# Early weight slots and tokens turned by VectorE in a one-core attention and mixture kernel

## The chip, the cores and the metric

One core of a Trainium2 chip runs the whole program. The metric is the device time of one execution in microseconds; lower is better. TensorE (PE) multiplies, VectorE (DVE), ScalarE (ACT) and GpSimd (POOL) do the work between, and SyncE (SP) issues most of the transfers, which 16 DMA engines carry out.

## The reference, cut to what matters

```python
scores = scale * np.matmul(q, k.transpose(0, 1, 3, 2)) - np.log(S)   # 4 batches, 12 heads, S = 448
x = (1.0 / (1.0 + np.exp(-scores))) @ v       # joined heads: 1792 tokens x 768
x = ((x @ w_a) * (x @ w_b)) @ w_out           # w_a, w_b: 768 x 1536; w_out: 1536 x 768
logits = x @ phi                              # 32 slots, 4 for each of 8 experts
d = softmax over all tokens of logits         # columns
slot_input = d.T @ x
slot_out[e] = relu(slot_input[e] @ w1[e]) @ w2[e]    # w1, w2: 8 x 768 x 1024 and 8 x 1024 x 768
out = softmax over slots of logits @ slot_out
```

All is 32-bit. The experts' weights w1 and w2 are 25.2 MB each; everything else is smaller.

## The kernel before

Four batches of 448 tokens pass through in order. `att` computes attention; `ab(0)` computes a * b for the first batch, between the steps of attention. For the two middle batches `unit(u)` (12 units of 7 block products, line 843) forms both batches' a and b at once; `put` multiplies them. `ab(B - 1)` does the last batch by itself: for each of 12 column blocks fc, and for a and b (i = 0, 1), 18 matmuls of 128 x 448 (line 660) in three sets of six. So it has 72 steps, counted by i in the main loop, with a `yield` after each set. w_a and w_b were rewritten to DRAM (`ab32`); each half block of 384 KB is loaded by `load_w` (line 542), rounded by DVE (line 550) and its low part formed by POOL (line 551). The load of fc 4's first half is the first that `run["load"]` asks for after the main loop has set up its buffers.

The product a * b of a column block lies with features on partitions (`gT`). To be summed over tokens it must lie with tokens on partitions (`gk`). `group(b, gi)` does this for four column blocks: for gi = 0 and 1 with DVE transposes of 32 x 32 pieces (line 603), then `store_gk` writes the result to DRAM (`gk32`, runs of 512 B) and `reload_gk` reads it back in token order; for gi = 2 with PE transposes (line 624) and copies out of PSUM (line 626), without DRAM. `LG(b)` then forms a batch's logits, their exponentials (`weights`) and, in `dg` (line 936), adds d.T @ (a * b) to `acc`. w_out is applied once, to that small sum. `fill` is a list of such pieces of side work; `fill_step` puts the next one into the program between sets of matmuls.

The experts' weights stream through a ring of slots of 8 KB per partition. `pump` takes the next of 61 pieces from `queue` (5 of w_out, 24 of w1 at 1 MB, 32 of w2 at 768 KB) and a free slot, and issues the load on SP; `done` frees a slot after its matmuls and pumps again. There are 22 slots in all: 17 in pool `e1` (its first six serve as reload buffers and work space until LG(1) and LG(2) are through), one `gkp`, and four `e2`, which open when `ab(B - 1)` has ended; the very last of them holds the last batch's gi = 2 tokens until `dg` of that batch. `e1` is opened at step 6 of `ab(B - 1)` in the memory of the block products, and the first `pump` comes at step 12. SP issues strictly in program order; an SP instruction that waits holds all loads behind it.

After `last_LG` comes the product with w_out (line 1229: four strips of 32 columns of PE, one for each fc modulo 4), then w1 (1249), w2 (1275) and the output (1301, 1323).

Of the kernel before, what the change touches and what calls it, by code (L numbers as in the profile page):

```python
# [20 lines left out]
C = 4  # L21
# [4 lines left out]
STARTS = (0, 128, 256, S - 128)  # L26
NP = H // 2
NE1, NE2 = 17, 4
# [12 lines left out]
def body(ctx, tc, q, k, v, w_a, w_b, w_out, phi, w1, w2, out):  # L41
# [5 lines left out]
    ps_ctx, ab_ctx, x0_ctx, cv_ctx, at_ctx, cp_ctx, xb_ctx = (ctx.enter_context(ExitStack()) for _ in range(7))  # L47
# [49 lines left out]
    gk32 = drp.tile([B, 2, S, 512], F32, name="gk32")  # L97
# [193 lines left out]
    def raw_x(b, kk):  # L291

        if b == 1 or (b == 3 and kk < 5):
            nm = f"t{kk if b == 1 else 6 + kk}"
            return x1p.tile([128, S], F32, tag=nm, name=nm)
        if b == 2 and kk >= 3:
            while fill:
                fill_step()
            return gT_all[kk - 1]
        nm = f"r{kk}" if b == 2 else "x3t"  # L300
        return pools["cp"].tile([128, S], F32, tag=nm, name=nm)
# [233 lines left out]
    LAST = 2 * (NCH - KF)  # L535

# [49 lines left out]

    def group(b, gi, evac=(act.copy, dve.tensor_copy) * 2):
# [12 lines left out]
        if gi < 2:  # L600
            turned = gk[:, :4 * S].rearrange("p (n f) -> p n f", f=128)
            for j in range(4):
                dve.transpose(turned[:, :, 32 * j:32 * j + 32], gT[b, 4 * gi + j].rearrange("p (n t) -> p n t", t=32))
                yield
                if b < B - 1:
# [32 lines left out]
    def store_gk(b, gi, turned, eng=sp, rows=range(4)):  # L638
        dst = gk32[b, gi].rearrange("(n t) (r f) -> r t n f", t=32, r=4)
        for r in rows:  # L640
            eng.dma_start(out=dst[r], in_=turned[32 * r:32 * r + 32])

    def reload_gk(b, gi, t):
        t = t.rearrange("p (c n) -> p c n", c=C)
        src = gk32[b, gi]
        sp.dma_start(out=t[:, :3], in_=src[:384].rearrange("(c p) n -> p c n", c=3))
        sp.dma_start(out=t[64:, 3], in_=src[384:])
        gtok[b, gi] = t

    def ab(b):  # L650
        for fc in range(KF):
# [3 lines left out]
            for i in range(2):  # L655
                wh, wl = ws[i]
                t = ps_tile("ab", [128, S], 2)
                for s, (w, xi) in enumerate(((wh, b == B - 1), (wh, b < B - 1), (wl, 0))):
# [23 lines left out]
                if LAST <= 2 * n + 2 < 2 * NCH:  # L682
# [8 lines left out]
                    if x + 1 == 2 * NCH:  # L691
                        run.pop("wr")
                        open_slots(run["e1"], [0])
                        pump()
# [11 lines left out]
    def load_u(u):  # L706
        if u > NU + 1:
            return
        t = pools["cp"].tile([128, 1536], F32, tag="wr", name="wr", bufs=2)
# [88 lines left out]
    def g_slot(u, q, n):  # L798
        k = (u // 2 * 4 + q) % 12
        while gslots.get(k) in live:  # L800
            fill_step()
        gslots[k] = n
        live.add(n)
        if k < 4:
            return gT_all[k + 1]
        if k < 8:
            return pools["xb"].tile([128, S], F32, tag=f"g{k}", name=f"g{k}")
        nm = ("r0", "r1", "r2", "x3t")[k - 8]
        return pools["cp"].tile([128, S], F32, tag=nm, name=nm)
# [3 lines left out]
    def p_tile():  # L813
        k = tmp[0] % 6
        tmp[0] += 1
        if 0 < tmp[0] - 1 < 4:
            nm = f"g{3 + k}"
            return pools["xb"].tile([128, S], F32, tag=nm, name=nm)
# [4 lines left out]
    def unit(u):  # L823
# [40 lines left out]
        if u % 4 == 3:  # L864
            fill.append(group(2, u // 4))
            fill.append(group(1, u // 4))
# [6 lines left out]
    def logits(b):  # L873
# [25 lines left out]
        ls, d = run["lsd"]  # L899
        if not b:  # L900
            dve.tensor_copy(ls, lf)
            run["exp"] = lambda: act.activation(d, ls, AF.Exp, bias=nm, accum_out=sm)
            run["s"] = sm
            return
        act.activation(d, lf, AF.Exp, bias=nm, accum_out=sm)
# [16 lines left out]
    def weights(d, dst):  # L922
        t = ms((128, C, NS))
        for c in range(C):
# [3 lines left out]
    def dg(b, dtok, gp, groups):  # L928

        kept = groups[0] == 2  # L930
        gk = gtok[b, groups[0]][:, None] if len(groups) == 1 else gk_01.rearrange("p g (c n) -> p g c n", c=C)
        o = gp.rearrange("p (g n) -> p g n", g=3)[:, groups[0]:groups[-1] + 1]
        for c in range(C):
            rows = slice(64 * (c == C - 1), 128)
            for j in range(4):
                pe.matmul(o[32 * j:32 * j + 32], dtok[rows, c], gk[rows, :, c, j * 128:(j + 1) * 128] if kept  # L936
                          else gk[rows, 0, c].rearrange("p (r j f) -> p j r f", r=4, j=4)[:, j],
# [18 lines left out]
    def rest_LG(b, dtok):  # L956
        weights(run["lsd"][1], dtok)
# [3 lines left out]
        for groups in ((0,), (1,), (2,)):  # L961
            dg(b, dtok, gp, groups)
# [5 lines left out]
        if b == B - 3:  # L968
            open_slots(run["e1"], [2, 3])
        elif b == B - 2:  # L970
            run.pop("lsd2")
            open_slots(run["e1"], [1, 4, 5])
# [13 lines left out]
    def last_LG():  # L986
# [9 lines left out]
        weights(run["lsd"][1], dtok)  # L996
# [4 lines left out]
        for groups in ((0,), (1,), (2,)):  # L1001
            dg(B - 1, dtok, gp, groups)
# [56 lines left out]
    def pump():  # L1059
# [6 lines left out]
        if what[0] == "wo":  # L1066
            i = what[1]
            if i < 3:
                t = t.rearrange("p (a n) -> p a n", a=4)
                src = out32[:, 4 * i:4 * i + 4, :512]  # L1070
            else:
                t = t[:, :6 * 256].rearrange("p (a n) -> p a n", a=6)
                src = out32[:, 6 * (i - 3):6 * (i - 3) + 6, 512:]
            sp.dma_start(out=t, in_=src)
# [55 lines left out]
    x0_ctx.close()  # L1130
    pools["cp"] = cp_ctx.enter_context(tc.tile_pool(name="cp", bufs=1, side="left"))
# [44 lines left out]
    load_w(LAST + 5)  # L1176
    for i, frac in enumerate(ab(B - 1)):
# [3 lines left out]
        if i == 6:  # L1181
            while fill:
                fill_step()
            cp_ctx.close()
            xb_ctx.close()
            e1 = run["e1"] = ctx.enter_context(tc.tile_pool(name="e1", bufs=1, side="right"))
            run["lsd2"] = e1.tile([128, 2048], F32, tag="e11", name="lsd2")
            run["wr"] = e1.tile([128, 2048], F32, tag="e10", name="wr")
            load_w(LAST + 6)
            load_w(LAST + 7)  # L1190
            for x in range(4):
                nm = f"e1{2 + x}"
                reload_gk(1 + x // 2, x % 2, e1.tile([128, 2048], F32, tag=nm, name=nm))
            open_slots(e1, range(6, NE1))
# [6 lines left out]
        if i >= 12 and i % 3 == 0:  # L1201
            pump()
# [20 lines left out]
    for what in order0:  # L1223
        i = what[1]
        h, n, f0 = (0, 4, 4 * i) if i < 3 else (1, 6, 6 * (i - 3))
        for x in range(n):
            fc = f0 + x
            j = fc % 4
            pe.matmul(sip[h][32 * j:32 * j + 32, :512 - 256 * h], GT[:, fc * NS:(fc + 1) * NS], ring[what][0][:, x],
                      start=(fc < 4), stop=(fc >= 8))  # L1230
# [118 lines left out]
```

## Time and profile before

| | |
|---|---|
| median of 3 runs | 664.79 us (662.77 to 665.39) |
| profiled execution | 664.73 us, its span 662.8 us |
| block products end, `ab(B - 1)` starts | 442.9 us |
| `ab(B - 1)` ends | 550.4 us |
| product with w_out starts | 561.6 us |
| last weights used, output written | 640 to 662.8 us |

Times in the rows are microseconds from the start of the span. Such a table gives the stations; what holds each stretch is read from the chain of waits and from the busy shares in that stretch.

### The profile page before, as it was taken

How to read it: one execution, taken by the hardware profiler on the slowest of the kernel's cores; microseconds unless marked ns; L12 is line 12 of the kernel's file. 1: busy time of each engine (PE TensorE's matmuls, PEld its weight loads, DVE VectorE, ACT ScalarE, POOL GpSimd, SP SyncE). 2: the span in 40 equal slices, each digit the busy share in tenths (PEclk: the TensorE clock that was granted, in tenths of full speed). 3: DMA queues.
4: the chain of work that ended last, by engine and by line, in shares of the span. 5: the costliest groups of instructions: out<-in, count | busy, mean ns of one | idle time of the engine just before them, and what ended most of it. 6: DMA issues, size and time to landing. Idle time of an engine off the chain costs nothing.

```text
span 662.8 us, 10904 instructions
## 1 busy us (share of the span) xinstructions
PE 633.0 (96%) x4015; PEld 449.9 (68%) x4015; DVE 380.1 (57%) x557; ACT 296.6 (45%) x534; POOL 308.4 (47%) x236
## 2 busy tenths in 40 slices
PE   6999999999999999999999999999999998997685
PEld 4557777777776555489988989888879895442121
DVE  4765797788774879588777766744324322200013
ACT  4888889889774677754423322202010002110022
POOL 0233676777644248579976575543334441000000
PEclk9999999999999999999999999999999999998798
DMA  9998999989968676501213423242999999999998
GB/s 204 280 258 221 298 305 291 314 268 300 278 166 184 112 150 143 179 1 47 96 49 103 111 89 101 69 134 80 347 372 333 384 369 344 410 415 416 409 374 303
DMA packets 145396, 154.25 MB, mean 233 GB/s; under 512 B 74336, under 2 KB 121792, under 8 KB 142272
## 3 DMA queue, kind: packets, MB, share of 16 engines
q1 hardware_dynamic: 138768, 150.01, 72.5%
q10 hardware_dynamic: 6576, 3.56, 1.9%
q8 instruction: 32, 0.52, 0.3%
q14 instruction: 20, 0.16, 0.1%
HBM read 126.36 MB, written 27.17 MB: 232 GB/s over the span
## 4 chain that ended last, share of the span: by engine, by line
PE 83%; DMA 11%; ACT 2%; DVE 2%; issue 1%; ACTq 1%; SPq 0%; DVEq 0%
PE ab L660 28%; PE sc L843 16%; DMA e<-in_moe_w 9%; PE sc L243 8%; PE ab L843 8%; PE sc L273 5%; PE ab L279 3%; PE ms L195 2%; PE ms L936 2%; PE ms L581 1%; DMA gkp<-in_moe_w 1%; PE ms L480 1%; PE ms L493 1%; PE ab L243 1%; ACT a L249 1%; PE ab L286 1%
## 5 line engine op out<-in xcount | busy, mean ns | idle before, releaser
L454 POOL TENSOR_TENSOR w<-gk,cy 128x768 int32<-128x768 int32 x36 | 66.2, 1842 | 80.1 <-DVE gk L449 35.3
L249 ACT ACTIVATE a<-sc,sums 112x448 f32<-112x448 f32 (+1 forms) x147 | 83.1, 650 | 15.8 <-PE sc L243 15.7
L660 PE MATMUL ab<-t,wh 128*128 128x448 f32 x288 | 65.1, 371 | 0.0
L660 PEld LDWEIGHTS ab<-t,wh 128*128 128x128 f32 x288 | 53.4, 188 | 6.1 <-issue 1.3
L551 POOL TENSOR_TENSOR wl<-wr,wh 128x768 fp32r<-128x768 f32 x16 | 29.5, 1841 | 49.7 <-DVE wh L550 31.9
L551 POOL TENSOR_TENSOR wl<-w,wh 128x768 fp32r<-128x768 f32 x24 | 45.0, 1878 | 10.1 <-ACT wh L550 10.1
L667 ACT COPY misc<-ab 128x448 f32<-128x448 f32 x24 | 12.7, 531 | 82.1 <-PE ab L660 75.2
L1275 PE MATMUL ab<-e,gk 128*32 128x384 f32 x240 | 34.3, 560 | 9.5 <-DMA e<-in_moe_w 9.5
L670 DVE TENSOR_TENSOR misc<-misc,ab 128x448 f32<-128x448 f32 x24 | 14.8, 616 | 43.9 <-PE ab L660 43.9
L273 PE MATMUL sc<-a,vn 112*64 112x448 f32 x192 | 38.7, 545 | 0.2 <-ACT a L249 0.2
L243 PE MATMUL sc<-qh,kh 64*112 64x448 f32 (+1 forms) x147 | 34.9, 447 | 1.0 <-ACT qh L183 0.6
L723 ACT CAST wx<-T 128x384 fp32r<-128x384 f32 x21 | 10.8, 513 | 55.7 <-DVE T L745 39.1
L660 PE MATMUL ab<-xh,wh 128*128 128x448 f32 x144 | 34.9, 377 | 0.0
L660 PE MATMUL ab<-xl,wh 128*128 128x448 f32 x144 | 34.7, 376 | 0.0
L724 POOL TENSOR_TENSOR wx<-T,wx 128x384 fp32r<-128x384 f32 x23 | 24.6, 1070 | 21.1 <-ACT wx L723 18.0
L660 PE MATMUL ab<-xh,wl 128*128 128x448 f32 x144 | 34.3, 373 | 0.0
L660 PE MATMUL ab<-t,wl 128*128 128x448 f32 x144 | 34.3, 373 | 0.0
L724 POOL TENSOR_TENSOR wx<-wr,wx 128x384 fp32r<-128x384 f32 x29 | 32.4, 1117 | 3.7 <-ACT wx L723 3.6
L1322 DVE COPY o<-sc 128x384 f32<-128x384 f32 x10 | 5.4, 554 | 48.2 <-PE sc L1301 47.0
L447 DVE TENSOR_SCALAR mf<-gk 128x768 f32<-128x768 f32 x24 | 22.7, 947 | 17.2 <-ACT gk L430 17.2
L660 PEld LDWEIGHTS ab<-xl,wh 128*128 128x128 f32 x144 | 25.9, 188 | 9.4 <-issue 7.7
L1275 PEld LDWEIGHTS ab<-e,gk 128*32 128x32 f32 x240 | 9.8, 120 | 32.8 <-DMA e<-in_moe_w 20.7
(492 smaller groups left out, 1526.6 us busy)
## 6 DMA issues: line engine op xcount, KB each, us to landing
e<-in_moe_w SPq DMA_DIRECT2D x23, 1024.0 KB, 8.5
e<-in_moe_w SPq DMA_DIRECT2D x23, 768.0 KB, 15.1
wr<-ab SPq DMA_DIRECT2D x14, 768.0 KB, 4.4
ab<-w SPq DMA_DIRECT2D x24, 384.0 KB, 6.4
gk<-gk SPq DMA_DIRECT2D x24, 224.0 KB, 4.0
e<-in_moe_w SPq DMA_DIRECT2D x14, 384.0 KB, 8.8
wr_cv<-in_moe_w_a SPq DMA_DIRECT2D x6, 768.0 KB, 7.9
wr_all<-in_moe_w_b SPq DMA_DIRECT2D x6, 768.0 KB, 6.8
```

Source lines behind the costliest of these rows:

```text
L243: pe.matmul(sc[h], kx[r, cs], qx[r], start=(i == 0), stop=(i == 2))
L249: act.activation(a, sc, AF.Sigmoid, bias=nlog[:n], scale=1.0 / math.sqrt(D))
L273: pe.matmul(pv[64 * h:64 * h + 64], qkv_t["v", g][:, h, c, :], a_t.pop((g, h, c)), start=(c == 0), stop=(c == C - 1))
L279: pe.matmul(pv[64 * h:64 * h + 64], qkv_t["v", g][:, h, c], a_t.pop((g, h, c)), start=(c == 0), stop=False)
L447: dve.tensor_scalar(mf, m, LOW, HIGH, op0=ALU.max, op1=ALU.min)
L454: pool.tensor_tensor(thirds(w), m.bitcast(I32), thirds(cy_t.pop(x)), op=ALU.add)
L551: pool.tensor_tensor(wl, t, wh.bitcast(F32), op=ALU.subtract)
L660: pe.matmul(t, w[:, kk * 128:(kk + 1) * 128], xt[b * NP + kk][xi], start=(s == 0 and kk == 0), stop=(s == 2 and kk == KD - 1))
L670: dve.tensor_tensor(g, g, t, op=ALU.mult)
L724: pool.tensor_tensor(w[:, 1], t, w[:, 0].bitcast(F32), op=ALU.subtract)
L843: pe.matmul(t, w[:, wi, k * 128:(k + 1) * 128], xs[ORDER[m], k][xi], start=(s == 0 and k == 0), stop=(s == 2 and k == 2))
L1275: pe.matmul(sps[h][32 * j:32 * j + 32], hT[:, 2 * x + i, 2 * j + g], ring[order2[n + j]][0][:, i, c0:c0 + w], start=(g == 0 and x == 0 and ...
```

## The change

`e1` (now 14 slots) is opened as soon as the block products have ended, and 8 of its slots are open to the ring from the first step; `pump` runs at every third step from step 0. What lives longer than the block products has a pool of its own (`hp`), whose memory becomes three further slots (`f1`) at step 6. The ring has 14 + 3 + 1 + 4 = 22 slots. For the middle batches (`TURNED`) also gi = 2 is turned by DVE and goes through DRAM; `gk32` is one tensor for each group, laid out so that a reload is one transfer of 112 rows of 8 KB, and each partition then holds four tokens that follow each other; `weights` and `dg` follow that order. Two reloads stand ahead of `ab(B - 1)`, four at steps 6 to 9. w_out is read in pieces of 8 KB rows, which cut across column blocks, so the product with it takes the pieces in that order. Some work tiles change places.

```diff
-NE1, NE2 = 17, 4
+NE1, NF1, NE2 = 14, 3, 4
...
+def turns(b, gi):
+    return gi < 2 or b in TURNED
...
-        if gi < 2:
+        if turns(b, gi):
...
     def reload_gk(b, gi, t):
+        if b in TURNED:
+            sp.dma_start(out=t[:T], in_=gk32[b][gi].rearrange("t n f -> (t n f)").rearrange("(p x) -> p x", p=T))
...
+    held_by = (None, KF + 8, 2 * KF + 9, 2 * KF + 8, KF + 9)
...
-                            while n - 5 in live or (n % KF == 4 and b and run["lg"] < b - 1):
+                            while n - 5 in live or (n % KF == 4 and b and run["lg"] < b - 1) or (b == B - 1 and held_by[n % 5] in live):
...
+            fill.append(group(1, u // 4))
             fill.append(group(2, u // 4))
-            fill.append(group(1, u // 4))
...
+    back = [(b, gi) for b in gtiles for gi in range(3)]
...
+    reload_next()
+    reload_next()
+    open_slots(e1, range(6, NE1))
     for i, frac in enumerate(ab(B - 1)):
...
-        if i >= 12 and i % 3 == 0:
+        if back and 6 <= i:
+            reload_next()
+        if i % 3 == 0:
             pump()
...
+        lo, hi = 2048 * what[1], min(2048 * what[1] + 2048, KF * DM)
+        cuts = [c for fc in range(KF) for c in (fc * DM, fc * DM + 512) if lo < c < hi]
+        for a, z in zip([lo] + cuts, cuts + [hi]):
+            fc, n0 = divmod(a, DM)
+            h, j = n0 // 512, fc % 4
+            n0 -= 512 * h
+            pe.matmul(sip[h][32 * j:32 * j + 32, n0:n0 + z - a], GT[:, fc * NS:(fc + 1) * NS],
```

Three places show where instructions stand. The first is SP's queue at the start of `ab(B - 1)`, of before; `gk_94` and `wr` are the halves of w_a and w_b (the first two rows are those of fc 2 and 3, the last is the first of fc 4), `e<-gk` the reloads, `e<-out` w_out.

```order
L542 DMA gk_94<-ab_99 128x768 x2
L542 DMA wr<-ab_99 128x768 x2
L646 DMA e_5063<-gk_102 128x3x512
L647 DMA e_5063<-gk_102 64x512
L646 DMA e_5066<-gk_102 128x3x512
L647 DMA e_5066<-gk_102 64x512
L646 DMA e_5069<-gk_102 128x3x512
L647 DMA e_5069<-gk_102 64x512
L646 DMA e_5072<-gk_102 128x3x512
L647 DMA e_5072<-gk_102 64x512
L542 DMA gk_94<-ab_99 128x768
L1074 DMA e_5141<-out_100 128x4x512
```

The same place after the change, from the first piece of w_out to the first half of fc 4 (`gk_94`); ahead of these rows stand the two halves of fc 2 and two reloads, `e_4953` and `e_4955`.

```order
L1084 DMA e_4964<-out_100 128x2048
L647 DMA gk_12_106<-gk_93 448x1x128 x4
L1084 DMA e_5004<-out_100 128x2048
L647 DMA gk_22_109<-gk_93 448x1x128 x4
L545 DMA wr<-ab_99 128x768 x2
L651 DMA e_5052<-gk_12_106 112x2048
L1084 DMA e_5054<-out_100 128x2048
L651 DMA e_5062<-gk_20_107 112x2048
L651 DMA e_5073<-gk_21_108 112x2048
L651 DMA e_5090<-gk_22_109 112x2048
L1084 DMA e_5092<-out_100 128x2048
L545 DMA gk_94<-ab_99 128x768
```

Where four reloads of 2 KB rows stood ahead of fc 4's first half, there now stand six reloads (two of them ahead of these rows), four pieces of w_out and two groups of four stores.

The second place is PE's product with w_out, of before; `e` are the five slots, and the two outputs `sc` are the columns 0 to 511 and 512 to 767.

```order
L1229 MATMUL sc_5956<-e16_5141,misc_95 32x512 x4
L1229 MATMUL sc_5956<-e17_5174,misc_95 32x512 x4
L1229 MATMUL sc_5956<-e18_5251,misc_95 32x512 x4
L1229 MATMUL sc_5957<-e19_5287,misc_95 32x256 x6
L1229 MATMUL sc_5957<-e110_5328,misc_95 32x256 x6
```

The first piece and a part of the second after the change.

```order
L1252 MATMUL sc_5937<-e16_4964,misc_95 32x512
L1252 MATMUL sc_5938<-e16_4964,misc_95 32x256
L1252 MATMUL sc_5937<-e16_4964,misc_95 32x512
L1252 MATMUL sc_5938<-e16_4964,misc_95 32x256
L1252 MATMUL sc_5937<-e16_4964,misc_95 32x512
L1252 MATMUL sc_5938<-e17_5004,misc_95 32x256
L1252 MATMUL sc_5937<-e17_5004,misc_95 32x512
```

Before, matmuls that follow each other go to the four strips in turn; now the two of one fc, which use the same strip, stand side by side, and the first slot is free after five matmuls instead of four.

## Rows read from the trace of the kernel before

**Rows 1.** The page: moved bytes per second in 40 equal slices of the span.

```profile
GB/s 204 280 258 221 298 305 291 314 268 300 278 166 184 112 150 143 179 1 47 96 49 103 111 89 101 69 134 80 347 372 333 384 369 344 410 415 416 409 374 303
```

**Rows 2.** The chain of waits, late part: start us, us, what.

```profile
494.59 27.47 PE ab L660 x132
...
561.64 4.08 PE sc L1229 x48
...
573.54 10.98 DMA e<-in_moe_w
```

**Rows 3.** Windows: PE, PEld, DVE, ACT, POOL busy (count), PE clock, DMA share, GB/s.

```profile
340.00:360.00 20.00, 20.00 (x102) 17.46 (x101) 13.59 (x21) 5.91 (x13) 12.54 (x13) 1.00 0.42 117
450.00:455.00 5.00, 5.00 (x35) 3.71 (x34) 1.53 (x3) 0.58 (x1) 1.84 (x1) 1.00 0.00 0
...
560.00:562.00 2.00, 1.24 (x11) 0.76 (x15) 0.99 (x4) 0.48 (x1) 0.93 (x2) 1.00 0.60 131
...
575.00:600.00 25.00, 23.95 (x206) 10.08 (x202) 2.08 (x3) 2.30 (x4) 0.00 (x0) 1.00 1.02 416
600.00:640.00 40.00, 29.27 (x186) 7.93 (x178) 0.00 (x0) 0.00 (x0) 0.00 (x0) 0.87 1.03 402
```

**Rows 4.** SP: what its queue waited for: us in total, times, longest.

```profile
SPq L1085 <- PE sc L1249: 8.8, 2, 7.0
SPq L1085 <- PE ab L936: 5.0, 1, 5.0
```

**Rows 5.** Timeline of PE at the start of `ab(B - 1)`: start us, us.

```profile
446.35 0.44 PE L624 MATMUL ms<-ident,g 128*128 128x128 f32 x2
...
446.76 1.47 PE L660 MATMUL ab<-t,wl 128*128 128x448 f32 x6
448.07 0.38 PE L624 MATMUL ms<-ident,g 128*128 128x128 f32 x2
...
448.86 1.46 PE L660 MATMUL ab<-t,wh 128*128 128x448 f32 x6
```

**Rows 6.** DVE's transposes and one copy out of PSUM.

```profile
L603 DVE STREAM_TRANSPOSE gk<-r x3: 630/633/636, 396.5 to 416.2; 128x448 f32<-128x448 f32 x3
450.80 0.69 DVE L626 COPY gk<-sc 128x512 f32<-128x512 f32 x1 [0.93 <-PE sc L624]
```

**Rows 7.** Timeline of SP.

```profile
408.83 3.00 SPq L641 DMA_DIRECT2D gk<-gk  x4
...
432.78 12.11 SPq L542 DMA_DIRECT2D gk<-ab  x2
458.48 0.80 SPq L542 DMA_DIRECT2D wr<-ab  x2
...
466.67 0.52 SPq L542 DMA_DIRECT2D gk<-ab  x1
```

**Rows 8.** Windows with one kind of transfer: 512 B stores, 3 KB, 2 KB and 8 KB reads.

```profile
411.00:412.00 1.00, 1.00 (x6) 0.92 (x6) 0.45 (x1) 0.00 (x0) 1.00 (x2) 1.00 0.87 176
...
436.00:437.00 1.00, 1.00 (x6) 0.93 (x5) 0.41 (x1) 0.00 (x0) 1.00 (x1) 1.00 1.03 384
...
465.00:470.00 5.00, 5.00 (x27) 4.36 (x26) 1.21 (x3) 0.53 (x1) 2.97 (x2) 1.00 1.03 320
...
576.00:578.00 2.00, 2.00 (x24) 0.58 (x20) 0.00 (x0) 0.00 (x0) 0.00 (x0) 1.00 1.02 422
```

**Rows 9.** When the weights of fc 4 and the reloads are used: DVE, then PE.

```profile
479.41 0.55 DVE L550 CAST wh<-gk 128x768 fp32r<-128x768 f32 x1
471.13 2.36 PE L936 MATMUL ms<-e,lsd 128*32 128x128 f32 x64
484.94 1.48 PE L660 MATMUL ab<-t,wh 128*128 128x448 f32 x6
```

**Rows 10.** Weight loads of the product with w_out on PE.

```profile
563.38 0.13 PEld L1229 LDWEIGHTS sc<-e,misc 128*32 128x32 f32 x4 [0.30 <-issue]
```

More of the change, by code (lines that the diff above doesn't have):

```diff
@@ L96, in body @@
     clog32 = drp.tile([T, C, B, NS], F32, name="clog32")
-    gk32 = drp.tile([B, 2, S, 512], F32, name="gk32")
+    gk32 = [[drp.tile([32, S // 32, 512] if b in TURNED else [S // 32, 32, 512], F32, name=f"gk32_{b}{gi}")
+             for gi in range(3 if b in TURNED else 2)] for b in range(B)]
     idj = ident.rearrange("p (j s) -> p j s", j=4)
@@ L604, in group @@
                 yield
-                if b < B - 1:
+                if b < B - 1 and gi < 2:
                     yield
@@ L692, in ab @@
                         run.pop("wr")
-                        open_slots(run["e1"], [0])
+                        open_slots(run["f1"], [0])
                         pump()
@@ L920, in tokens, with weights @@
         dve.tensor_copy(dst, t)
-    def weights(d, dst):
+    def weights(b, d, dst):
         t = ms((128, C, NS))
+        if b in TURNED:
+            for c in range(C):
+                pe.transpose(t[:T, c], d[:NS, c::C], ident[:NS, :NS])
+            dve.tensor_copy(dst[:T], t[:T])
+            return
         for c in range(C):
@@ L956, in rest_LG @@
     def rest_LG(b, dtok):
-        weights(run["lsd"][1], dtok)
+        weights(b, run["lsd"][1], dtok)
         for _ in range((3, 4, 1)[b]):
@@ L960, in rest_LG @@
         gp = ms((128, FF // 4))
-        for groups in ((0,), (1,), (2,)):
-            dg(b, dtok, gp, groups)
+        for gi in range(3):
+            dg(b, dtok, gp, gi)
         if b:
@@ L967, in rest_LG @@
         yield
-        if b == B - 3:
-            open_slots(run["e1"], [2, 3])
-        elif b == B - 2:
+        if b == B - 2:
             run.pop("lsd2")
-            open_slots(run["e1"], [1, 4, 5])
+            open_slots(run["f1"], [1])
+        if b:
+            open_slots(run["e1"], gtiles[b])
     def first_LG():
@@ L995, in last_LG @@
         dtok = wphi[:, 4:4 + C]
-        weights(run["lsd"][1], dtok)
+        weights(B - 1, run["lsd"][1], dtok)
         for _ in gr:
@@ L1000, in last_LG @@
         gp = ms((128, FF // 4))
-        for groups in ((0,), (1,), (2,)):
-            dg(B - 1, dtok, gp, groups)
+        for gi in range(3):
+            dg(B - 1, dtok, gp, gi)
         dve.scalar_tensor_tensor(acc, acc, run["al"], gp, op0=ALU.mult, op1=ALU.add)
@@ L1176, in body, with reload_next @@
     load_w(LAST + 5)
+    cp_ctx.close()
+    xb_ctx.close()
+    e1 = run["e1"] = ctx.enter_context(tc.tile_pool(name="e1", bufs=1, side="right"))
+    back = [(b, gi) for b in gtiles for gi in range(3)]
+    def reload_next():
+        b, gi = back.pop(0)
+        nm = f"e1{gtiles[b][gi]}"
+        reload_gk(b, gi, e1.tile([128, 2048], F32, tag=nm, name=nm))
+    reload_next()
+    reload_next()
+    open_slots(e1, range(6, NE1))
     for i, frac in enumerate(ab(B - 1)):
@@ L1183, in body @@
                 fill_step()
[L1184 to L1188, printed above, removed]
+            hp_ctx.close()
+            f1 = run["f1"] = ctx.enter_context(tc.tile_pool(name="f1", bufs=1, side="right"))
+            run["lsd2"] = f1.tile([128, 2048], F32, tag="f11", name="lsd2")
+            run["wr"] = f1.tile([128, 2048], F32, tag="f10", name="wr")
             load_w(LAST + 6)
             load_w(LAST + 7)
[L1191 to L1194, printed above, removed]
+            open_slots(f1, [2])
             fill.append(LG(1))
@@ L1223, in body @@
     for what in order0:
[L1224 to L1230, printed above, removed]
+        lo, hi = 2048 * what[1], min(2048 * what[1] + 2048, KF * DM)
[5 more added lines that the diff above has]
+            pe.matmul(sip[h][32 * j:32 * j + 32, n0:n0 + z - a], GT[:, fc * NS:(fc + 1) * NS],
+                      ring[what][0][:, a - lo:z - lo], start=(fc < 4), stop=(fc >= 8))
         done(what)
```

52 lines of the change are left out of this document (25 added, 27 removed).

## The prediction

> **What bounds the kernel now.** The page's bytes per second come first [rows 1]: from about 465 us on the transfers run at 330 to 416 GB/s to the end, so one suspects that whatever starts them earlier ends the kernel earlier. The chain of waits says the same only for the last part [rows 2]: up to 561.64 it is PE work, one set of matmuls behind the other (132 of them in 27.47 us, 0.208 us each), the product with w_out follows, and from 573.54 it is the loads of the experts' weights. The windows decide [rows 3]. From 575 to 640 the transfers run at 416 and 402 GB/s with a share of 1.02 and 1.03, and nothing can be added there. But at 560 to 562 they fall to 131 GB/s with a share of 0.60: at that moment the ring is full. 21 of its 22 slots are loaded, and SP stands still, because the last slot holds tokens that `dg` of the last batch still reads; SP waited 5.0 us for that [rows 4]. So the clock of the end starts when PE has finished this `dg` at about 560. From there 40 pieces are left (8 of 1.049 MB, 32 of 0.786 MB: 33.5 MB), which at 409 GB/s take 82 us, to 642, close to the 640 at which the trace has them used. The rest is output.
>
> What counts is therefore when PE gets to 560. From 443 it hardly rests: the windows of the block products and of `ab(B - 1)` have PE at their full length, at a granted clock of 1.00, which is 2.4 GHz [rows 3].
>
> **The change part by part, against the profiled execution of 664.73 us (the median of the runs, 664.79, is the same).**
>
> *Slots open at the block products' end.* The transfers stand idle at 450 to 455 (share 0.00, [rows 3]), and the stream now fills such gaps, some 17 us of them before its first load at 458.5 [rows 7]. At the end this is worth 0: the number of slots is still 22, the last one still waits for the same `dg`, and the ring was already full when it was needed. The stream only becomes full earlier and waits.
>
> *Turning by DVE.* 32 PE transposes leave the stretch 446 to 457. They stand in six places; the first two take 446.35 to 446.76 and 448.07 to 448.86, 0.41 and 0.79 us [rows 5], and the six together 0.41 + 0.79 + 0.35 + 0.41 + 0.79 + 0.35 = 3.1 us. Four of the places vanish altogether, and each change of the kind of work costs a little: the six matmuls from 446.76 to 448.07 take 1.31 us where six at 0.208 take 1.25. I take 0.07 for each, so PE gains 3.4 us. In their place DVE gets eight transposes of 0.633 us and loses four copies of 0.69 [rows 6], 2.3 us more; ACT loses four copies. DVE is busy 1.53 of 5 us there [rows 3], and the two halves of fc 1 that it must round come after them with about 1 us to spare; if that were gone PE would wait for the excess alone. Below 0 nothing speaks for a cost on PE.
>
> *Two store groups and six reloads.* They hang on the transfers' queue, and behind them hangs the first half of fc 4's weights, whose place the order rows show. Durations from windows with one kind of transfer [rows 8]: 8 KB rows 422 GB/s, so 2.5 us for a piece of w_out and 2.2 for a reload of 0.918 MB; 384 KB of weights at 384 GB/s, 1.0; stores in 512 B runs 176 GB/s at a share of 0.87, so 202 at a full share and 4.5 us for four of 0.229 MB. The queue is taken up when fc 2's second half, issued at the end of the row that starts at 432.78 [rows 7], has landed at about 447. Then come two reloads 4.4, four pieces of w_out 10.0, two store groups 9.0, two weight halves 2.0, four reloads 8.8 and fc 4's half 1.0: 35.2 us, landing at 482.2. Each waiting SP instruction there is issued while the queue has work (the stores wait for DVE until about 450 and 455, when the loads ahead are not through before 454 and 461), so the queue never runs dry. DVE's rounding takes 0.55 [rows 9], so the weights are ready at 482.8 to 483.5. PE needed them at 484.94 and comes 3.4 us earlier, at 481.5. In the kernel before, this load was issued at 466.67 [rows 7] and DVE had it rounded from 479.41 [rows 9], 5 us ahead of its use; now it is late by 1.3 to 2.0. I take 1.8. DVE, which stands still in that wait, holds back the second logits too, but PE reaches them behind the same matmuls. The third group of batch 1, which is now read back, is through at 447 + 4.4 + 5.0 + 9.0 + 2.0 + 2.2 = 469.6; PE comes to `dg` at 471.13 - 3.4 = 467.7 and to its third part 2.36 us later [rows 9], 470.1. It is hidden by 0.5 us; if not, its lateness is not added to fc 4's, which then shrinks. After fc 4 each column block needs 2 weight halves and 2 pieces (7.0 us) per 7.5 us of PE, so nothing is late again; the ring is full earlier, and the last halves, which were tight, have the queue to themselves.
>
> *w_out in 8 KB rows.* 4.7 MB at 422 instead of 320 GB/s saves 3 us of the queue, which the sum above has. The product itself has the same columns in 25 matmuls instead of 24. Before, four strips work together: four weight loads in each 0.43 us [rows 10]. Now both matmuls of an fc sit on one strip, and no row shows how far PE looks past a busy strip. Lower bound 0; for the upper bound see the third rival. I take 0, since the next slot is needed later than PE frees it.
>
> *Without a price.* `dg` has as many matmuls, on 112 rows; `weights` as many transposes; the exponential writes another order, where ACT is busy 0.58 of 5 us. Swapping the groups and work tiles in the block products leaves DVE 13.59 of 20 us and PE full [rows 3]; a late tile there could cost some tenths.
>
> **Sum:** 664.73 - 3.4 + 1.8 = **663.1 us**. A change under 0.5% (3.3 us) can't be told from none here.
>
> **Rivals.**
>
> 1. *Nothing is late.* If the stores overlap with the reads, fc 4's half lands before 480.9 and the full 3.4 us remain: 661.3. For it: reads of 8 KB leave room. Against: a share of 0.87 in the store window [rows 8] is an almost full queue. The Trainium skill (DMA: Bandwidth & Descriptors, Specifications) puts the smallest transfer at line rate at 512 B. By that, the two store groups would take 4.3 us instead of 9.0, and fc 4's half would land at 477.5. The trace disagrees: 512 B runs went at 176 GB/s [rows 8].
>
> 2. *The queue is later still, slower than before.* The place is the same wait of fc 4's half. If the mixed queue runs as it did at 465 to 470, 320 GB/s [rows 8], its 10.4 MB without the stores take 32.5 us instead of 26.2, and with the stores at 176 GB/s without the share, 10.4 instead of 9.0, the half lands at 489.9 and is used from 490.5: 9.0 us of wait, 670.3. It decides from a landing at 484.3 on, where the wait eats the whole 3.4, and is measurable from 487.6. For it: writes and reads share the engines, which no row shows with 8 KB rows. Against: 8 KB rows gave 422.
>
> 3. *The product with w_out loses its strips.* If PE doesn't look past a busy strip, each fc takes its four passes in turn (each matmul goes through twice: 2 x 0.43 + 2 x 0.21), about 1.07 us until the next strip starts, 12.8 us for twelve instead of 4.08 [rows 2]. Slots of w1 are then free 6 to 8.7 us later. SP waited 7.0 us for the first of them [rows 4], to about 573, with five pieces (12.5 us) issued from 562.8 on, which last to about 579; less 2 us for the way of a transfer, some 4 us were to spare, so the end moves by 2 to 4.7: 665 to 668. The Trainium skill (TensorE: Matmul & The Clock Gate, Part 3) has matmuls in strict program order, in start and end. By that this rival holds. No row here has two matmuls on one strip in a row, so the trace can't yet say.
>
> 4. *The early stream does end earlier.* If the ring weren't full at 560, up to 17 us could be won: about 648. Against it stands 131 GB/s at 560 to 562 [rows 3].
>
> **How the numbers follow.** Forecast (late by 1 to 3 us, 662 to 665.5) 0.5; rival 1 0.18; rival 2 0.17; rival 3 0.1; rival 4 0.05. Rival 1 is faster by over 0.5% (under 661.5) in two thirds of its cases, rival 4 in all; with a little for gains that I don't see, faster 0.2. Rival 2 is over 668.1 in most of its cases, rival 3 at its far end: slower 0.15. Same 0.65. The range leaves out rival 4 and the far half of rival 2: 660.2 to 669.
>
> **What would show it.** Right: PE without transposes at 443 to 460 and its sets of matmuls after that some 3.4 us earlier; then a PE gap of about 2 us before the first matmul of fc 4, ended by DVE's rounding, which waits for DMA; transfers dense from 445 and nearly idle somewhere between 535 and 560; the product with w_out starting 1 to 2 us before 561.6, and the same 80 us from there. Wrong: no gap at fc 4 (rival 1), a gap over 4 us or others after it (rival 2), the product with w_out over 6 us long and a dip in the transfers near 575 (rival 3), or a ring that still loads without a dip at 560 (rival 4).

## The result, and the profile after

The changed kernel takes 673.16 us (median of 5 runs, 672.50 to 676.60) against 664.79: a ratio of 1.0141, 95% interval 1.0108 to 1.0173. By the medians it is 8.4 us slower (7.2 to 11.5 by the interval); 663.1 and a range to 669 had been forecast. The profiled execution took 672.5 us, its span 670.7. Of all executions reported below one, of e10, took 1004.23 us at a granted clock of 0.56; it is left out of its row.

First the timeline of PE after the change, around `dg` of batch 1 (L952) and fc 4 (columns as in [rows 5]; in brackets the idle time ahead of an instruction and what ended it).

```profile
467.59 1.95 PE L952 MATMUL ms<-e,lsd 112*32 112x128 f32 x64
473.35 1.94 PE L952 MATMUL ms<-e,lsd 112*32 112x128 f32 x32 [3.81 <-DMA e<-gk]
475.21 2.18 PE L672 MATMUL ab<-t,wl 128*128 128x448 f32 x6
...
491.76 2.61 PE L672 MATMUL ab<-t,wh 128*128 128x448 f32 x6 [5.26 <-DVE wh L553]
494.30 4.22 PE L952 MATMUL ms<-e,lsd 112*32 112x128 f32 x96
```

The gain on PE is there: `dg` starts at 467.59 and not at 471.13 [rows 9]. Then PE waits twice, 3.81 us for the third reload of batch 1 and 5.26 us for fc 4's weights, and works slowly behind both: six matmuls take 2.61 us that took 1.48 [rows 9]. Fc 4 begins 6.8 us later than before.

Windows of the same kernel (columns as in [rows 3]) show what the transfers and the clock do.

```profile
465.90:469.40 3.50, 3.50 (x73) 2.98 (x71) 0.56 (x1) 0.00 (x0) 0.00 (x0) 1.00 0.55 171
...
477.00:480.00 3.00, 3.00 (x14) 2.45 (x14) 1.69 (x3) 0.00 (x0) 1.28 (x1) 1.00 1.02 262
481.00:484.00 3.00, 3.00 (x16) 2.63 (x15) 0.00 (x0) 1.96 (x5) 0.00 (x0) 1.00 0.98 240
...
473.35:475.30 1.95, 1.95 (x33) 1.48 (x33) 0.00 (x0) 0.00 (x0) 0.00 (x0) 0.50 1.04 403
...
491.80:495.80 4.00, 4.00 (x35) 3.18 (x39) 1.70 (x5) 0.00 (x0) 3.41 (x2) 0.50 1.02 416
...
545.00:550.00 5.00, 5.00 (x27) 4.63 (x26) 1.07 (x1) 0.53 (x1) 3.48 (x2) 1.00 0.46 127
...
580.00:640.00 60.00, 47.93 (x391) 18.09 (x384) 3.58 (x7) 2.30 (x4) 0.00 (x0) 0.97 1.02 412
```

While only reloads run (477 to 480, 481 to 484) the 16 engines are busy all the time and move 262 and 240 GB/s, where 8 KB rows had given 422 [rows 8]. At 465.9 to 469.4 the queue is half empty. Behind each wait the granted clock is 0.50, that is 1.2 GHz. At 545 to 550 the ring is full and the transfers half rest, and from 580 on they run at 412 GB/s, as before [rows 3].

SP's queue in that stretch (start us, us, the instruction):

```profile
444.65 0.84 SPq L651 DMA_DIRECT2D e<-gk  x2
...
448.98 4.71 SPq L647 DMA_DIRECT2D gk<-gk  x4
...
462.10 4.98 SPq L545 DMA_DIRECT2D wr<-ab  x2
467.14 0.42 SPq L651 DMA_DIRECT2D e<-gk  x1
...
470.45 0.37 SPq L545 DMA_DIRECT2D gk<-ab  x1
```

Inside the row of 462.10, SP waits for a store of logits that ScalarE issued (us in total, times, longest):

```profile
SPq L545 <- DMA clog<-lsd: 3.7, 1, 3.7
```

And the chain of waits:

```profile
461.20 5.54 DMA clog<-lsd
...
470.45 20.58 DMA gk<-ab
...
503.26 26.94 PE ab L672 x132
...
569.27 4.62 PE sc L1252 x40
```

The last row of SP's queue is the first half of fc 4. It is issued at 470.45 and lands 20.58 us later, at 491.0, behind everything that stands ahead of it in the queue. From there to the end hardly anything more is lost: the first long set of 132 matmuls starts at 503.26, 8.7 us later than at 494.59 [rows 2], the product with w_out 7.6 us later, and the span ends 7.9 us later.

### The profile page after: what moved, and what is told of

The parts are those of the page before. It is cut to its first block, busy times and chain, and to the rows that moved or that the text cites. A ratio compares the mean times of both kernels' runs of the same rounds, so it can differ in the third digit from the quotient of the medians.

```text
span 670.7 us, 10844 instructions
## 1 busy us (share of the span) xinstructions
PE 629.7 (94%) x3985; PEld 451.5 (67%) x3985; DVE 384.6 (57%) x561; ACT 295.0 (44%) x530; POOL 307.9 (46%) x236
## 4 chain that ended last, share of the span: by engine, by line
PE 80%; DMA 11%; DVE 3%; ACT 2%; SPq 1%; issue 1%; POOL 1%; ACTq 1%; DVEq 0%
PE ab L672 25%; PE sc L854 16%; PE ab L854 7%; PE sc L245 7%; PE sc L275 5%; PE sc L1272 3%; DMA gk<-ab 3%; DMA e<-in_moe_w 2%; DMA f<-in_moe_w 2%; PE ab L281 2%; PE ms L197 2%; PE ms L584 1%; DMA gkp<-in_moe_w 1%; PE ms L482 1%; PE ms L952 1%
## 5 line engine op out<-in xcount | busy, mean ns | idle before, releaser
L1298 PE MATMUL ab<-e,gk 128*32 128x384 f32 x200 | 31.1, 529 | 9.0 <-DMA e<-in_moe_w 9.0
L672 PEld LDWEIGHTS ab<-t,wl 128*128 128x128 f32 x144 | 27.3, 192 | 5.0 <-issue 2.2
## 6 DMA issues: line engine op xcount, KB each, us to landing
e<-in_moe_w SPq DMA_DIRECT2D x20, 1024.0 KB, 10.1
```

Of the source, the lines that this page charges most:

```text
L672: pe.matmul(t, w[:, kk * 128:(kk + 1) * 128], xt[b * NP + kk][xi], start=(s == 0 and kk == 0), stop=(s == 2 and kk == KD - 1))
L1298: pe.matmul(sps[h][32 * j:32 * j + 32], hT[:, 2 * x + i, 2 * j + g], ring[order2[n + j]][0][:, i, c0:c0 + w], start=(g == 0 and x == 0 and ...
```

## The experiments

Every kernel is the changed one with the edit shown, unless it says otherwise. "Half" is the landing of fc 4's first half of weights in the profiled execution; "waits" are PE's idle times for loads up to 500 us, and then from 500 to 550. The kernel before ran again beside each series (medians 663.9 to 664.4), and the ratios are to those runs. Landings include where the stretch began: fc 2's second half, ahead of it all, lands at 447.7 in the changed kernel, 446.1 in e7, 452.4 in e13 and 446.8 to 448.1 in the others.

| | median us | ratio to before (95%) | half | waits to 500; later |
|---|---|---|---|---|
| changed kernel | 673.16 | 1.0141 (1.0108 to 1.0173) | 491.0 | 3.8, 5.3; none |
| e1_rows128 | 670.55 | 1.0107 (1.0079 to 1.0136) | 489.2 | 2.8, 2.1; none |
| e2_spread | 674.34 | 1.0159 (1.0143 to 1.0175) | 492.1 | 5.1, 4.4; none |
| e3_wout_late | 671.25 | 1.0112 (1.0095 to 1.0129) | 483.7 | 4.3; 0.3, 2.3 |
| e4_before_8k | 664.68 | 1.0009 (1.0000 to 1.0019) | | none |
| e5_rows128_full | 670.46 | 1.0105 (1.0085 to 1.0125) | 487.7 | 3.1, 1.2; none |
| e6_clog_late | 676.88 | 1.0196 (1.0166 to 1.0226) | 496.2 | 5.9, 7.4; none |
| e7_same_bytes | 667.15 | 1.0044 (1.0028 to 1.0059) | 484.2 | 2.0, 1.3; none |
| e8_filler | 671.88 | 1.0119 (1.0104 to 1.0135) | 492.2 | filled; none |
| e9_all | 665.78 | 1.0033 (1.0016 to 1.0049) | 478.6 | none; 0.4, 2.2, 1.1 |
| e10_two_ahead | 667.51 | 1.0045 (1.0028 to 1.0061) | 481.2 | none; 2.7, 1.5 |
| e11_seven | 673.04 | 1.0121 (1.0095 to 1.0146) | 479.4 | none; none |
| e12_seven_three | 673.76 | 1.0131 (1.0096 to 1.0166) | 482.4 | none; none |
| e13_strips | 668.24 | 1.0066 (1.0035 to 1.0097) | 484.6 | none; 4.7, 0.8 |
| e14_pool | 665.24 | 1.0009 (0.9998 to 1.0021) | 480.2 | none; 0.4, 1.2 |
| e15_three | 666.79 | 1.0041 (1.0028 to 1.0054) | 482.1 | none; none |
| e16_two_pool | 664.49 | 1.0001 (0.9989 to 1.0014) | 480.3 | none; 1.7, 0.6 |
| e17_one_pool | 663.42 | 0.9978 (0.9965 to 0.9991) | 477.3 | none; 0.3 |
| e18_three_pool | 665.88 | 1.0015 (0.9998 to 1.0032) | 483.1 | 2.2; none |

In e11 to e15 PE also stands still just ahead of fc 4 for a small operation of VectorE, which the table leaves out: 0.4, 0.4, 1.2, 1.0 and, in e15, 3.9 us.

The theory after the first look (A): a reload of 112 rows is slow in itself, and fc 4's half stands behind six of them. The rivals: the source is slow (B), SP holds the loads back by its own waits (C), and, for what comes behind the waits, PE's clock (D).

**e1_rows128**: 384 tokens on 128 partitions, 64 on half of them (weights and `dg` follow).

```diff
-sp.dma_start(out=t[:T], in_=...rearrange("(p x) -> p x", p=T))
+sp.dma_start(out=t[:, :1536], in_=src[:384].rearrange("(p c) n -> p (c n)", c=3))
+sp.dma_start(out=t[64:, 1536:], in_=src[384:])
```

> The changed kernel, but a reload lands on 128 partitions (384 tokens as 128 rows of 6 KB, the other 64 as rows of 2 KB) instead of 112 rows of 8 KB; same bytes, same DRAM layout, same place in the queue. Theory A (a transfer to 112 rows is slow in itself: 3.1 to 3.7 us for 0.918 MB in the changed kernel): a reload takes about 2.3 us, the first half of fc 4's weights lands at about 485 instead of 491.0, PE's wait there falls from 5.3 to under 1 us, the wait in dg of batch 1 from 3.8 to about 2.6, total about 665 us. Theory B (the source is slow: 0.918 MB that lies in one piece in DRAM and was just written): reloads stay at 3.1 to 3.7 us, total about 673.

It moved the right way and only a third as far: 315 GB/s in this window of reloads.

```profile
479.80:482.00 2.20, 2.20 (x11) 1.71 (x11) 1.01 (x4) 0.00 (x0) 1.29 (x1) 1.00 1.05 315
```

**e2_spread**: 112 rows read from the copy of w_out.

```diff
-in_=gk32[b][gi].rearrange("t n f -> (t n f)").rearrange("(p x) -> p x", p=T)
+in_=out32.rearrange("p k n -> p (k n)")[:T, :2048]
```

> The changed kernel, but the six reloads of 112 rows of 8 KB read their rows from the copy of w_out in DRAM, 36 KB apart, as the loads of w_out do, instead of from the stored a * b; the tokens of the middle batches are therefore left out of the sum. Theory A (112 rows are slow whatever they are read from): reloads stay at 3.1 to 3.7 us, fc 4's half lands at about 491, total 673 within 1. Theory B (the source is slow): reloads take 2.2 us, fc 4's half lands at about 485, total about 665.

Nothing became faster, so theory B falls: rows 36 KB apart, from which 128-row loads run fast, come as slowly into 112 partitions.

```profile
477.00:480.00 3.00, 3.00 (x11) 2.67 (x10) 1.03 (x3) 0.00 (x0) 0.00 (x0) 0.57 1.03 257
481.00:484.00 3.00, 3.00 (x16) 2.69 (x15) 1.03 (x4) 0.26 (x1) 1.14 (x1) 1.00 1.02 251
```

**e3_wout_late**: `if i % 3 == 0: pump()` becomes `if i >= 12 and i % 3 == 0: pump()`.

> The changed kernel, but the first piece of w_out is asked for at step 12 instead of step 0, so that no w_out stands ahead of fc 4's first half; reloads as changed. Theory A and theory B alike (the queue ahead of that half is too long; four pieces of w_out are 10 us of it): fc 4's half lands at 480 to 483, PE's wait there is 0 to 2 us, the wait in dg of batch 1 under 1.5 us, total 661 to 664. Theory C (SP stands still in waits on its own, not the transfers): fc 4's half is issued as late as in the changed kernel, total 670 to 673.

The half lands 7.3 us earlier, and PE's wait for the third reload is gone; but the wait at fc 4 is still 4.3 us, and weights are late again at 536 and 542 (0.3 and 2.3 us, the second with slow matmuls behind it). The half is issued at 470.11, hardly earlier than before the edit (470.45), and the total is in theory C's range, not in that of A and B. SP's waits say that reloads stood 9.1 us behind ScalarE's store of logits (L965), and towards the end of that the transfers stood still:

```profile
SPq L651 <- DMA clog<-lsd: 9.1, 1, 9.1
...
467.00:469.00 2.00, 2.00 (x80) 2.00 (x81) 0.00 (x0) 0.00 (x0) 0.00 (x0) 1.00 0.04 14
```

So with a short queue the hold of theory C costs time; e6 asks what it does in the changed kernel.

**e4_before_8k**: the kernel before with w_out in 8 KB runs and its product in that order.

> The kernel before with one part of the change alone: w_out read in 8 KB runs, and its product in the order that this gives. Theory: nothing was late behind w_out there, so earlier loads are worth nothing, and the product on PE takes 4.6 us instead of 4.1 as in the changed kernel: 664.8 to 665.4 us. Rival (the 8 KB runs themselves gain, since the ring fills earlier): under 663.

664.68, just under the range. This part of the change gains nothing by itself and costs at most 0.2% (1.3 us); its product takes 4.62 us on PE here too.

**e5_rows128_full**: the second part of the reload of e1 takes `src[S - 128:]` to all partitions.

> The changed kernel with reloads that use all 128 partitions in both parts (128 rows of 6 KB, and 128 rows of 2 KB for the last tokens, 64 of them read a second time; 1.049 MB in place of 0.918). Theory A (a transfer is slow when its rows aren't 128): a reload takes 2.5 to 2.7 us, less than the 3.0 to 3.2 with a part of 64 rows and the 3.1 to 3.7 with 112 rows although it moves more; fc 4's half lands at 486 to 488, total 668 to 670. Rival (only the number of bytes counts, or mixing kinds of transfers): 3.5 us or more for a reload, total 673 or more.

A window of reloads shows 400 GB/s, the half lands at 487.7; the median is just above its range, and the profiled execution (668.4) is the fastest of four.

```profile
479.00:481.00 2.00, 2.00 (x9) 1.55 (x8) 0.75 (x2) 0.00 (x0) 1.39 (x1) 0.94 1.02 400
```

**e7_same_bytes**: the cleanest test of A.

```diff
-sp.dma_start(out=t[:T], in_=....rearrange("(p x) -> p x", p=T))
+sp.dma_start(out=t[:, :1792], in_=....rearrange("(p x) -> p x", p=128))
```

> The changed kernel with nothing altered but the split of a reload: the same 0.918 MB from the same place as one transfer of 128 rows of 7 KB instead of 112 rows of 8 KB. The tokens then lie otherwise than the weights of dg expect, and dg reads 448 columns for a token's 512, so the sum over the middle batches is left out. Theory A (it is the 112 rows): a reload takes 2.2 to 2.4 us, the pieces of w_out between them stay at 2.5, fc 4's half lands at 484 to 486 instead of 491, total 667 to 669. Rival (the bytes, the source or the neighbours in the queue make it): reloads at 3.1 to 3.7 us, total 673.

Same bytes, same source, same single transfer: 427 and 422 GB/s in windows of reloads, five of the six reloads 2.2 to 2.5 us (one 3.1), the half at 484.2, 667.15 us. This queue began 1.6 us earlier, so of the 6.9 us that the half gained 5.2 are the stretch's own. The edit also shortens the rows to 7 KB, but the length of the rows is not the reason: the pieces of w_out have rows of 8 KB, 36 KB apart, as the reloads of e2 have, and the last one ahead of fc 4's half, 128 of these rows, takes 2.3 us in the changed kernel and in e2. Theory A stands.

```profile
476.00:478.00 2.00, 2.00 (x11) 1.71 (x10) 1.20 (x4) 0.00 (x0) 1.50 (x1) 1.00 1.04 427
479.00:480.00 1.00, 1.00 (x7) 0.93 (x6) 0.00 (x0) 1.00 (x2) 0.00 (x0) 1.00 1.01 422
```

**e6_clog_late**: the logits' stores of both middle batches are kept until the end of `rest_LG(2)`.

```diff
-(act if b else sp).dma_start(out=clog32[:, :, b], in_=ltok[:T])
+run.setdefault("ltok", []).append(ltok)
```

> The changed kernel, but the two stores of logits that ScalarE issues within this stretch (448 runs of 128 B each; the first at 461.2, landed 466.7) are both issued after the second dg, so that no load of SP has to wait for one. Reloads and order of the queue as changed. Theory C (SP's load of fc 3's second half is held from 462.1 to 466.8 by the landing of the logits' store, and the queue runs empty): that load is issued by 463, no window between 465 and 470 falls under a share of 0.9, fc 4's half lands at 487 to 488, total 668.5 to 670.5. Rival (another landing holds SP just as long, or the 112-row reloads alone make the lateness): total 672 to 674.

SP's load is issued at 462.05 instead of 466.76 and the queue no longer runs empty, but the half lands 5.2 us later (the profiled execution, 678.5, is one of the two slower ones of four; the other two took 675.0 and 675.2). With more of them outstanding, the 112-row reloads are slower still, and so is the piece of w_out between them (first row):

```profile
477.00:480.00 3.00, 3.00 (x15) 2.39 (x8) 0.61 (x1) 0.00 (x0) 0.00 (x0) 0.50 1.02 216
...
482.00:485.00 3.00, 3.00 (x15) 2.62 (x14) 1.00 (x4) 0.19 (x1) 1.12 (x1) 1.00 1.02 213
486.00:489.00 3.00, 3.00 (x18) 2.21 (x16) 0.00 (x0) 0.78 (x4) 0.00 (x0) 1.00 1.05 208
```

So theory C falls for the changed kernel: the hold was real and not what made fc 4 late. In e3, where less stood on the queue, it did cost.

**e8_filler**: `filler(18)` ahead of the third part of batch 1's `dg`, `filler(33)` ahead of fc 4, matmuls of x by itself.

> The changed kernel with idle work for PE in its two waits: 18 matmuls of 128x448 ahead of the third part of the first dg and 33 ahead of fc 4, whose result nobody reads, about as long as the waits. The landing of fc 4's half stays at about 491, so its first matmul stays at about 491.8. Theory D (after each wait PE is granted half its clock for some us, which costs 1.8 us behind fc 4): granted clock 1.00 from 470 to 500, the 11.50 us from the first matmul of fc 4 to the first long set of 132 become 9.65, total 671.3. Rival (PE is slow there for another reason, as weights that come late): 11.5 us again, total 673.

Timeline of PE, where L665 is the filler, and a window behind it (columns as in [rows 3]).

```profile
485.82 6.96 PE L665 MATMUL ms<-t 128*128 128x448 f32 x33
492.93 1.50 PE L679 MATMUL ab<-t,wh 128*128 128x448 f32 x6
494.36 2.83 PE L959 MATMUL sc<-e,lsd 112*32 112x128 f32 x96
...
490.00:495.00 5.00, 4.85 (x44) 3.93 (x46) 2.08 (x6) 0.00 (x0) 1.85 (x1) 1.00 1.04 418
```

The granted clock stays at 1.00. The six matmuls take 1.50 instead of 2.61, `dg` 2.83 instead of 4.22, and from the first matmul of fc 4 to the first long set it is 8.99 us instead of 11.50. Theory D holds, with 2.5 us and not 1.8. The half landed 1.2 us later in this kernel, so the total shows only a part of it.

**e9_all**: e5, e6 and `pump` at steps 0 and from 12 on.

> The changed kernel with three things undone or mended at once: reloads on 128 partitions (6 KB and 2 KB rows), the logits' stores after the second dg, and only one piece of w_out ahead of fc 4's first half instead of four. Theories A, C and the order of the queue together: fc 4's half lands by 481, PE waits nowhere for over 0.5 us from 443 to 560, granted clock 1.00, total 660 to 662. If a wait remains at fc 4, the theories leave a cause out: 664 or more.

The first half of it came: the half at 478.6, no wait up to 500, fc 4 at 481.53 instead of 484.94 [rows 9]. But PE gave it back later, in three waits for weights that had not been there before:

```profile
532.49 2.66 PE L674 MATMUL ab<-t,wh 128*128 128x448 f32 x12 [0.36 <-DVE wh L553]
538.60 2.69 PE L674 MATMUL ab<-t,wh 128*128 128x448 f32 x12 [2.23 <-DVE wh L553]
543.64 2.67 PE L674 MATMUL ab<-t,wh 128*128 128x448 f32 x12 [1.13 <-DVE wh L553]
```

So a cause had been left out. Theory E: the queue is too full there, more must be read early. Theory F: SP's loads are held by the landing of the last batch's stores (`gk<-gk`), which ScalarE issues. SP's waits from 500 to 560 show such a hold ahead of the late loads:

```profile
SPq L1103 <- DMA gk<-gk: 7.7, 1, 7.7
```

**e10_two_ahead**: `pump` also at step 6.

> As the kernel with three things mended, but a second piece of w_out is asked for behind batch 1's third reload. There, with one piece ahead, PE lost nothing up to 500 and then 3.7 us in three waits for weight halves between 530 and 545, each landing 8 us after its issue. Theory E (the queue is full to 545 in that order too: what is not read ahead of 480 comes in front of the later halves): fc 4's half lands at 481, PE waits under 0.5 us there, the three later waits fall together to 1 to 2 us, total 663 to 665. Rival (the later waits come from something else, as ScalarE's stores at 496 to 506): they stay at 3.7 us, total 665.8.

Against E: the waits grew to 4.1 us. The chain of waits names a store of ScalarE ahead of the late load:

```profile
523.58 10.95 DMA gk<-gk
534.97 6.43 DMA wr<-ab
```

**e11_seven** and **e12_seven_three**: the last 64 tokens as halves on 128 partitions, with two and three pieces ahead.

> As the kernel with two pieces of w_out ahead, but a reload takes its 0.918 MB as 128 rows of 6 KB and 128 rows of 1 KB (the last 64 tokens lie as halves on 128 partitions, with a second set of weights in dg), so that no byte is read twice: 0.8 MB less in the queue, about 2 us. dg has 8 more short matmuls for each group and VectorE three more small operations in each set of weights. Theories A and E: fc 4's half lands at 479, later waits of PE 0 to 1 us in all, total 661 to 663.5; rival (the 1 KB rows cost as much as the 2 KB rows did): 663 to 665.

> As the kernel with the 6 KB and 1 KB rows, but a third piece of w_out ahead of fc 4's half. Theory E: that half lands at 481.5 to 482, PE waits 0 to 1 us there, and nowhere later: total 660.5 to 663. If the half lands later than 483, PE waits over 1.5 us, its clock falls behind the wait, and the total is 664 or more.

673.04 and 673.76 us: in both, each `dg` took 8.5 us, since the new loop did a strip's five matmuls one behind the other. The chain of e11 from the first `dg` matmul to the next set:

```profile
467.62 0.77 PE ms L963 x6
...
476.15 2.62 PE ab L676 x12
```

**e13_strips**: the loops swapped, strips inside.

```diff
-for j in range(4):
-    for c in range(C - 1): pe.matmul(o[32 * j:32 * j + 32], dtok[:, c], ...)
+for c in range(C - 1):
+    for j in range(4): pe.matmul(o[32 * j:32 * j + 32], dtok[:, c], ...)
```

> As the kernel with 6 KB and 1 KB rows and two pieces of w_out ahead, but dg goes through the four strips of PE in turn, as all kernels but the last two did (there each strip got its five matmuls one behind the other, and a dg took 8.5 us instead of 3.4). Theory G (matmuls that follow each other on one strip are done one after the other, those on four strips together): a dg takes 3.4 to 3.8 us again, PE is at the long sets of 132 at 491 to 492, total 664 to 666 with the later waits that the kernel with two pieces ahead has. Rival (the short matmuls or the second set of weights make dg slow): dg stays over 6 us, total over 668.

The same matmuls take 2.8 us (its chain: 472.87 to 475.65), so theory G holds. Its profiled execution was already 5 us behind when the block products ended, so of its times only lengths are compared.

```profile
472.87 0.79 PE ms L963 x24
...
475.65 2.63 PE ab L676 x12
```

**e14_pool** and **e15_three**: the last batch's stores by GpSimd (`store_gk(b, gi, turned, pool, (r,))`), and a third piece ahead.

> As the kernel before this one in the list, but the eight stores of the last batch's turned products are issued by GpSimd instead of ScalarE. In the kernel with two pieces of w_out ahead, a load of weights by SP was held until such a store had landed (523.6 to 535.0), and PE waited behind it. Theory F (SP's loads are held by the landing of stores that ScalarE issued, since both share what counts their landings): PE's waits from 500 to 560 fall under 1 us in all, total 661 to 663.5. Theory E alone (the queue is simply too full there): the waits stay at 2 to 4 us, total 664 to 666. GpSimd may also be late with the low halves of the weights, as it has to issue: then waits ended by GpSimd show, total over 665.

> As the kernel before this one in the list, with a third piece of w_out ahead of fc 4's half. Theory E: fc 4's half lands at 481.5 to 482.5, PE waits 0.3 to 1.3 us there, and less later than with two: total 661 to 663. If only theory F counts, total is within 1 us of the kernel with two pieces.

665.24 and 666.79 us. The later waits fell from 5.5 us (e13) to 1.6, and to none with a third piece; but with that the half landed at 482.1, VectorE stood still for it for 7.0 us, and PE then waited 3.9 us for VectorE ahead of fc 4.

**e16_two_pool, e17_one_pool, e18_three_pool**: e10, e9 and three pieces ahead, with GpSimd's stores.

> The kernel with the reloads of 128 rows in 6 KB and 2 KB, the logits' stores behind the second dg and two pieces of w_out ahead (667.7 us, PE waits of 2.7 and 1.5 us between 530 and 545), with the last batch's eight stores issued by GpSimd instead of ScalarE. Theory F (SP's loads of weights are held there by the landing of ScalarE's stores): those waits fall to under 1 us in all, dg of the last batch ends at 557 to 558, total 662 to 664. Theory E alone (the queue is too full): waits stay at 3 to 4 us, total 666 to 668.

> The same with one piece of w_out ahead instead of two (665.8 us with ScalarE's stores, PE waits of 0.4, 2.2 and 1.1 us). Theory F: waits under 1.5 us in all, 662.5 to 664.5; theory E adds about 1 us against the kernel with two pieces.

> The same with three pieces of w_out ahead. Theory of the queue ahead of fc 4: its half lands at 483 to 484, PE waits 1.5 to 2.5 us there and has half its clock for some us behind it, no waits later: 664 to 666, slower than with two.

The stores alone moved: e9 to e17 is 665.78 to 663.42, e10 to e16 667.51 to 664.49. PE's later waits fall from 3.7 to 0.26 us and from 4.1 to 2.35, and SP's loads no longer wait for these stores. Theory F holds for most of it in e9's order, for not quite half in e10's. Theory E has a part that is right: with three pieces ahead (e15, e18) no later wait is left. But then fc 4 waits, from one piece to two the later waits grow, and in total fewer pieces are better. Why 2.35 us stay in e16 is open. In e17 the long sets and the product with w_out stand at

```profile
490.71 27.47 PE ab L674 x132
...
558.13 4.62 PE sc L1260 x40
```

3.9 and 3.5 us earlier than before [rows 2], and its one late wait is

```profile
539.37 2.67 PE L674 MATMUL ab<-t,wh 128*128 128x448 f32 x12 [0.26 <-DVE wh L553]
```

It is the only kernel here that is faster than the kernel before: 0.9978, by 0.1 to 0.35%. Its profiled execution, 661.9 us, is one of its fastest, so the 3 us between the two spans (662.8 and 659.8) are more than the medians' 0.9.

## Why the prediction was wrong

**The bound** was right. The product with w_out starts at 561.64, 569.27, 562.41 and 558.13 in the kernel before, the changed one, e9 and e17, and their spans end 101.2, 101.4, 101.2 and 101.7 us after it. In e3, e11, e13 and e14 it was 102.8 to 103.4, which no run explains. Opening slots early filled the gaps and gained nothing at the end, as forecast; the transfers half rested at 545 to 550, and no run has this part alone.

**PE's gain** was right: 3.4 us forecast; 3.5 at the first `dg`, 3.4 at fc 4 in e9.

**The step that failed is the sum of the queue**, "35.2 us, landing at 482.2". It landed at 491.0, 43.3 us after fc 2's second half (447.7). Its terms, by landings:

- *Reloads 2.2 us each, "8 KB rows 422 GB/s".* They took 3.1 to 3.7 each, six of them 7.5 us more than forecast. The row with 422 had 128 partitions; the reload has 112, which the prediction passed over. e7 shows that this made them slow, and e2 that it isn't the source; by the medians e7 takes back 6.0 of the 10.1 us between forecast and result. The Trainium skill (SBUF — State Buffer, Door 1: The DMA port swizzle) has 16 ports of eight partitions each, and (DMA: Bandwidth & Descriptors, The descriptor swizzle) one engine for each port in a transfer of 128 partitions. No run here shows ports, and why 112 rows are slow stays open.
- *Stores 4.5 us for a group of four.* They took 3.1 and 2.9 behind full transfers. The row used had a share of 0.87 and one group alone.
- *Pieces of w_out 2.5 us each.* The four took 13.4 us, not 10.0; the longest, 5.0, ran beside the second group of stores.
- *"[...] the queue never runs dry."* It did, at 465.9 to 469.4, as SP waited for a store of ScalarE that the sum didn't have. e6 shows that this did not decide.

So 482.2 + 7.5 (reloads) + 3.4 (w_out) - 3.0 (stores) + 0.3 (weight halves) + 0.7 (a later start) is 491.1.

**The wait of 1.8 us** was the right place with the wrong size: fc 4 starts at 491.76, 10.3 us behind the 481.5 at which PE could have come. The third reload of batch 1, "hidden by 0.5", landed at 473.3 instead of 469.6 and was waited for; that wait lies inside the lateness of fc 4, as forecast.

**A term was missing**: the clock behind a wait, 2.5 us by e8. At full clock the stretch from fc 4 to the first long set takes 8.99 us (e8), 0.7 less than before (9.65), most of it because `dg` on 112 rows takes 2.83 us and not 3.4, a gain that the prediction left without a price. So that stretch adds 11.50 - 9.65 = 1.85. The sum is 664.7 - 3.4 + 10.3 + 1.9 = 673.5; 1.1 go off because the two long sets took 26.94 instead of 27.47 us each, which no run explains. That gives 672.4; the profiled execution took 672.5.

**That "nothing is late again"** after fc 4 held in the changed kernel. It failed where fc 4 came early: e9 lost 3.7 us to weights between 530 and 545.

**The rivals.** Rival 2 gave this place, a landing at 489.9 and 670.3, and its sign, a gap of over 4 us, came; it was held at 0.17, and its own reason (stores and mixed reads) was not the cause, so its nearness is luck. Its bytes are 10.9 MB and not 10.4 (six reloads, four pieces and three halves), with which its own sum gives 491.4. Rival 1's price came out where nothing was late, in e17, whose product starts 3.5 us earlier. Rival 3: the product took 4.62 us instead of 4.08 and cost nothing (e4); but in e11 the order of strips in `dg` cost 5.7 us each time (8.5 against 2.8 in e13). The Trainium skill (TensorE: Matmul & The Clock Gate, Part 3) has matmuls start and end in program order. By that the first matmul for a free strip can't pass those that queue ahead of it on a busy one, and e11 against e13 agrees. Rival 4 had nothing.

## What to carry to other kernels

Take a transfer's rate from a row with the same number of partitions, not only the same run length: here 112 rows of 8 KB cost half as much again as 128 rows of 7 KB, and in e6 the piece of w_out between them ran at 216 GB/s too. When a late load is the risk, count everything ahead of it on its queue, and price the wait with the slow clock behind it. A gain on the engine that bounds is kept only if every later load keeps up: here it took the order of the queue, the shape of the reloads and another issuer of the stores together, and 0.9 of 3.4 us was left in the median.

## What the runs showed of the hardware

- The same 0.918 MB: 240 to 262 GB/s into 112 partitions, 422 to 427 into 128, at a DMA share of about 1.0 in both. Part on 64 partitions (e1): 315. With more outstanding, 112-row reloads fell to 208 to 213 (e6).
- Behind most waits of PE, of 1.3 (e7) to 7.4 us (e6), the mean granted clock was 0.50 to 0.63 in the stretch of some 4 us that followed; behind one of 1.2 us in e5 it was 1.00, and so behind 1.5 (e10), 1.7 (e16) and 2.2 us (e9). Of two waits of 2.2 to 2.3 us, one (e3) was followed by twelve matmuls in 4.26 us and the other (e9) by twelve in 2.69. What tells them apart is open.
- SP's loads can stand behind the landing of a store that ScalarE issued: 3.7 us in the changed kernel, 9.1 in e3, 7.7 in e9. In the changed kernel the trace's records have the store and the load that waits for it on the same semaphore. Moved to GpSimd, the last batch's stores no longer held them.
